# Shifting one key chunk of every second tile from TensorE's transposes to the DMA transposes, with the keys stored in load order

## The chip, the cores and the metric

One core of a Trainium2 chip runs the whole kernel as one program. Its engines are TensorE (PE; its weight loads are PEld), VectorE (DVE), ScalarE (ACT), GpSimd (POOL) and SyncE (SP), which here only issues DMAs. The metric is device time in microseconds. The kernel before took 1773.42 us (median of three runs, 1768.99 to 1776.42).

## The reference

Two stages follow each other. The first is attention of 49152 query rows (4 batches of 12288, 128 channels) over 768 keys per batch, which are 4 x 4 means of a larger array, projected; keys and values are the same rows. The second is a mixture of eight experts: a skip score decides which rows are computed, the best of eight logits chooses the expert, and two products (128 to 1024 to 128) with a ReLU between them are scaled and added to the row.

```python
kv_flat = kv.reshape(B, H // 4, 4, W // 4, 4, C).mean(axis=(2, 4)).reshape(B, -1, C) @ w_sr
k = v = kv_flat
a = softmax(q @ k.transpose(0, 2, 1) / sqrt(C))       # 12288 x 768 per batch
x = (a @ v).reshape(B * S, C)
do_compute = x @ w_skip > 0
e_idx = argmax(xc @ w_gate)                           # xc: the rows with do_compute
h = maximum(xc[mask] @ w1[e], 0.0)
y[mask] = gate_w[mask, None] * (h @ w2[e])
out[do_compute] = xc + y                              # other rows: out = x
```

## The kernel before

**Attention** runs over 384 tiles of 128 queries, 96 to a batch. The keys of a batch stand in six chunks of 128. One step `t` of the loop issues work of several tiles at once, and every engine executes its instructions in the order in which the step lists them:

- `p_transpose(t - 2)`, then `scores(t)`: six products of 384 columns, L637 to L639, which stand for one product of the scores in three parts (high by high, high by low, low by high);
- `attend(t - 10)`: 18 products of 138 columns, L700. Each needs a transposed 128 x 128 block of the tile's probabilities as its weights, for six key chunks, a high and a low part of each;
- `row_max(t)` on VectorE (L645), `row_exp(t)` on ScalarE (L650), and `p_hi(t - 1)` on ScalarE (L654) and `p_lo(t - 1)` on VectorE (L658), which split the probabilities of some chunks into two f16 parts.

The transposed probabilities come by two ways. The first `KD = 4` key chunks are split in SBUF (`p16`, 128 x 1024 f16) and transposed by one DMA per tile, which SyncE issues at L661 into `pt`. The other two chunks are transposed by TensorE in f32 (L674, two 128 x 128 products for a tile). Two tiles (`PP = 2`) share one PSUM bank for that, and it is split into `ptq` once for the pair, on ScalarE (L682) and VectorE (L683). `attend` takes its weights from `pt` and `ptq`. It runs ten steps after the scores (`LAG = 10`); `ptp` has 10 buffers for `pt`, `hl` 9 for `p16`, `ptq` 6.

**The keys of the next batch** are loaded while a batch is worked on. Each of the six chunks takes four loads of 256 KB (128 partitions of 2 KB): one plain load that SyncE issues (L448) and three that GpSimd issues and that add to what is there (L450). `KV_T` spreads the 24 loads over the first 75 tiles of a batch. GpSimd then adds up the rest (L476, L479), and `prep_kv` projects the keys. The keys of the first batch are loaded ahead of the loop, 24 plain loads, which VectorE (L463) and GpSimd pool as they land.

**SyncE's queue** holds, in program order, the DMA transposes, the loads of the queries (L602, one for four tiles), the stores of the attention rows (L719, one for four tiles) and the plain key loads. GpSimd issues the adding key loads and the writes of routed rows into expert buckets (L194).

**The experts.** The first group of rows is worked on ahead of a loop (`peel`), from buffers that are named `up_ps` on TensorE. Then `n_it` is read (the number of iterations, L1063) and the loop of groups begins, whose first instruction on TensorE is L293.

The lines of the change and of the prediction's steps:

Of the kernel before, what the change touches and what calls it, by code (L numbers as in the profile page):

```python
# [9 lines left out]
F32 = mybir.dt.float32  # L10
F32R = mybir.dt.float32r
BF16 = mybir.dt.bfloat16
F16 = mybir.dt.float16
# [11 lines left out]
def kernel(  # L25
# [11 lines left out]
    nc = tc.nc  # L37
    NR, C, RT, P = q.shape
    B = kv.shape[0]
    NQ = NR * RT * P // B  # L40
    H, W = kv.shape[1], kv.shape[2]
    R = 4
    NK = (H // R) * (W // R)
    KC = NK // P
# [24 lines left out]
    W1, W2, W3 = 3, 6, 0  # L69
    PSL = 11  # L70
    KD = 4
    PP = 2
# [334 lines left out]
    with ExitStack() as p1:  # L407
# [31 lines left out]
        W8 = W // R  # L439
        HG = P // W8  # L440
# [211 lines left out]
        def p_hi(t):  # L652
            P16[t] = hl.tile([P, 2, KD * P], F16, name="p16")
            nc.scalar.activation(out=P16[t][:, 0, :], in_=p_flat(t)[:, 0:KD * P], func=AF.Copy, scale=2.0 ** PEXP)  # L654

        def p_lo(t):
            p16 = P16.pop(t)
            LO[:] = [nc.vector.scalar_tensor_tensor(out=p16[:, 1, :], in0=p_flat(t)[:, 0:KD * P], scalar=2.0 ** PEXP,  # L658
                                                    in1=p16[:, 0, :], op0=ALU.mult, op1=ALU.subtract).ins]
            PT[t] = ptp.tile([P, 2 * KD, P], F16, name="pt")  # L660
            nc.sync.dma_start_transpose(PT[t], p16.rearrange("p a x -> p (a x)"))  # L661
# [4 lines left out]
        KP = KC - KD  # L666

        def p_transpose(t):
            g, j = divmod(t, PP)
            if j == 0:  # L670
                PTP[g] = acc_ps()
            p = p_flat(t)
            for i in range(KP):
                nc.tensor.transpose(PTP[g][:, (j * KP + i) * P:(j * KP + i + 1) * P],  # L674
                                    p[:, (KD + i) * P:(KD + i + 1) * P], ident)
            P_SB.pop(t)
            if j < PP - 1:
                return
            ps = PTP[g][:, 0:PP * KP * P]
            hl_t = ptq.tile([P, 2, PP * KP * P], F16, name="ptq")  # L680
            PTQ[g] = hl_t.rearrange("p a (j k x) -> p a j k x", j=PP, x=P)
# [6 lines left out]
        def attend(t):  # L688
# [8 lines left out]
            ptq_t = PTQ[t // PP]  # L697
            for i, (k, a, x) in enumerate(AVL):
                w = pt[:, x * KD + k, :] if k < KD else ptq_t[:, x, t % PP, k - KD, :]
                nc.tensor.matmul(ps[:, j % 2, :], w, v[a][:, k, :], start=(i == 0), stop=(i == len(AVL) - 1))  # L700
# [362 lines left out]
        n_it = nc.values_load(cumi[0:1, 0:1], min_val=1, max_val=NG + 1)  # L1063

# [70 lines left out]
```

## Time and profile before

| | |
|---|---|
| median of the runs | 1773.42 us |
| profiled execution | 1778.48 us, of which the traced span is 1776.7 |
| TensorE busy | 1721.4 us, 97% |
| VectorE, ScalarE, GpSimd busy | 85%, 74%, 36% |
| attention tiles | about 40 to 992 us |
| first group of the experts | 992 to 1026 us |
| loop over groups | from 1028 us |

The profile is one execution. Its matmuls overlap, so their durations add up to more than the time that they take: what one product costs TensorE is read from the distance between starts. "DMA share" is the time of all packets over the time of 16 DMA engines. It goes over 1.00 where an engine works on several packets at once, so that 1.00 is not its limit. A DMA's duration in the SyncE rows is the time of its issue: it grows where SyncE has to wait until the queue takes more.

### The profile page before, as it was taken

Reading aid. Unit: us, or ns where it says so; the run is one execution under the profiler, and the core shown is the slowest. Engines: PE = TensorE matmul, PEld = TensorE weight load, DVE = VectorE, ACT = ScalarE, POOL = GpSimd, SP = SyncE. Lnnn points to the kernel's source line nnn. Section 1 sums busy time; section 2 is a strip of 40 time slices with the busy share of each in tenths; the row PEclk is TensorE's granted clock in tenths of the full one; section 3 lists DMA queues with packets and bytes.
Section 4 is the critical chain, followed back from the end, with each engine's and each line's share of the span. In section 5 each row is a group of like instructions: output and inputs, shape, how many; then the busy total and the mean of one; then the engine's idle time right before and its main releaser. Section 6 shows DMA issues by size and latency. Waiting matters only on the chain. (4 is left out here: it accounts for less than half of the span.)

```text
span 1776.7 us, 41426 instructions
## 1 busy us (share of the span) xinstructions
PE 1721.4 (97%) x13906; PEld 1240.2 (70%) x13906; DVE 1502.7 (85%) x3181; ACT 1317.0 (74%) x2487; POOL 632.0 (36%) x799
## 2 busy tenths in 40 slices
PE   3999999999999999999999999999999999999997
PEld 2899989999899999999988544444444444444443
DVE  6888889899899988999999678888888788888886
ACT  2888888888888888888898456666666666666664
POOL 3233423444334344232332133333333333333333
PEclk9999999999999999999999999999999999999999
DMA  7999999999999999999999233333333433333333
GB/s 186 181 209 216 219 212 234 223 215 202 223 226 226 202 230 235 210 167 231 231 182 207 78 102 96 96 96 101 101 98 98 101 97 96 97 104 99 98 103 82
DMA packets 609811, 284.83 MB, mean 160 GB/s; under 512 B 495616, under 2 KB 564352, under 8 KB 609664
## 3 DMA queue, kind: packets, MB, share of 16 engines
q1 hardware_dynamic: 588064, 222.76, 63.9%
q0 software_dynamic: 21600, 60.19, 12.9%
q8 instruction: 83, 1.36, 0.3%
q14 instruction: 64, 0.52, 0.1%
HBM read 90.47 MB, written 72.30 MB: 92 GB/s over the span
## 5 line engine op out<-in xcount | busy, mean ns | idle before, releaser
L297 DVE SCALAR_TENSOR_TENSOR h_lo<-h_ps,h_hi 128x512 f16<-128x512 f32 x544 | 344.1, 685 | 134.9 <-ACT h_hi L296 134.9
L186 POOL DMA_INDIRECT out_dram<-o,ids x288 | 283.2, 983 | 478.9 <-DVE o L328 410.1
L650 ACT ACTIVATE p_sb<-s_ps,nm 128x768 f32<-128x768 f32 x384 | 347.4, 905 | 115.8 <-DVE nm L645 112.9
L645 DVE TENSOR_REDUCE nm<-s_ps 128x1 f32<-128x768 f32 x384 | 365.2, 951 | 69.7 <-PE s_ps L639 66.3
L296 ACT ACTIVATE h_hi<-h_ps 128x512 f16<-128x512 f32 x544 | 318.1, 597 | 49.7 <-PE h_ps L295 30.2
L700 PE MATMUL acc_ps<-v_hi,pt 128*128 128x138 f16 x3072 | 320.1, 224 | 5.3 <-DMA pt<-p 5.1
L700 PEld LDWEIGHTS <-pt 128*128 128x128 f16 x4608 | 275.2, 97 | 67.5 <-issue 55.7
L700 PE MATMUL acc_ps<-v_lo,pt 128*128 128x138 f16 x1536 | 293.0, 223 | 0.0
L637 PE MATMUL s_ps<-k_hi,q_hi 128*128 128x384 f32 x768 | 291.8, 380 | 0.0
L658 DVE SCALAR_TENSOR_TENSOR p<-p_sb,p 128x512 f16<-128x512 f32 x384 | 273.7, 713 | 3.0 <-ACT p L654 2.7
L619 POOL TENSOR_TENSOR q_lo<-q_sb,q_hi 128x256 fp32r<-128x256 f32 (+1 forms) x190 | 147.8, 779 | 327.2 <-DVE p L658 195.6
L639 PE MATMUL s_ps<-k_hi,q_lo 128*128 128x384 f32 x768 | 258.9, 337 | 0.0
L638 PE MATMUL s_ps<-k_lo,q_hi 128*128 128x384 f32 x768 | 258.0, 336 | 0.0
L654 ACT ACTIVATE p<-p_sb 128x512 f16<-128x512 f32 x384 | 243.1, 633 | 10.1 <-DMA pt<-p 7.3
L293 PE MATMUL h_ps<-xT,w_hi 128*128 128x512 f16 x544 | 207.1, 381 | 2.7 <-issue 2.7
L294 PE MATMUL h_ps<-xT,w_hi 128*128 128x512 f16 x544 | 207.2, 381 | 0.0
L295 PE MATMUL h_ps<-xT,w_lo 128*128 128x512 f16 x544 | 207.1, 381 | 0.0
L309 PEld LDWEIGHTS <-w_hi 128*128 128x128 f16 x1152 | 112.7, 98 | 134.9 <-issue 1.5
L309 PE MATMUL y_ps<-h_hi,w_hi 128*128 128x512 f16 x544 | 206.2, 379 | 0.0
L309 PE MATMUL y_ps<-h_hi,w_lo 128*128 128x512 f16 x544 | 206.2, 379 | 0.0
L312 ACT ACTIVATE yT<-y_ps,y_sc 128x512 f32<-128x512 f32 x68 | 46.7, 687 | 214.7 <-PE y_ps L309 155.7
L309 PE MATMUL y_ps<-h_lo,w_hi 128*128 128x512 f16 x544 | 195.1, 379 | 0.0
(214 smaller groups left out, 2932.1 us busy)
## 6 DMA issues: line engine op xcount, KB each, us to landing
q_sb<-in_q_dram SPq DMA_DIRECT2D x96, 256.0 KB, 4.8
out_dram<-rows SPq DMA_DIRECT2D x96, 256.0 KB, 3.7
xin<-scr SPq DMA_DIRECT2D x75, 276.0 KB, 3.0
w_raw<-in_moe_w_dram SPq DMA_DIRECT2D x34, 512.0 KB, 3.8
kvt<-in_kv_dram POOLq DMA_DIRECT2D x54, 256.0 KB, 5.8
kvt<-in_kv_dram SPq DMA_DIRECT2D x42, 256.0 KB, 5.4
pt<-p SPq DMA_TRANSPOSE x384, 4.7
out_dram<-o,ids POOLq DMA_INDIRECT x288, 2.7
```

Source lines behind the costliest of these rows:

```text
L186: ins = nc.gpsimd.indirect_dma_start(out=dst, out_offset=bass.IndirectOffsetOnAxis(ap=ids, axis=0), in_=src, in_offset=None, bounds_check= ...
L296: nc.scalar.activation(out=h["hi"][:, c, :], in_=ps, func=AF.Relu)
L297: nc.vector.scalar_tensor_tensor(out=h["lo"][:, c, :], in0=ps, scalar=0.0, in1=h["hi"][:, c, :], op0=ALU.max, op1=ALU.subtract)
L309: nc.tensor.matmul(ps, w[:, c, :], h[x][:, c, :], start=(i == 0), stop=(i == len(terms) - 1))
L637: nc.tensor.matmul(s[:, h, :HK], q_hi, k_hi[:, sl], start=True, stop=False)
L638: nc.tensor.matmul(s[:, h, :HK], q_hi, k_lo[:, sl], start=False, stop=False)
L639: nc.tensor.matmul(s[:, h, :HK], q_lo, k_hi[:, sl], start=False, stop=True)
L645: nc.vector.tensor_reduce(out=NM[t], in_=S_PS[t][:, :, :HK], axis=AX.XY, op=ALU.max, negate=True)
L650: nc.scalar.activation(out=P_SB[t], in_=S_PS.pop(t)[:, :, :HK], func=AF.Exp, bias=NM.pop(t))
L654: nc.scalar.activation(out=P16[t][:, 0, :], in_=p_flat(t)[:, 0:KD * P], func=AF.Copy, scale=2.0 ** PEXP)
L658: LO[:] = [nc.vector.scalar_tensor_tensor(out=p16[:, 1, :], in0=p_flat(t)[:, 0:KD * P], scalar=2.0 ** PEXP, in1=p16[:, 0, :], op0=ALU.mult ...
L700: nc.tensor.matmul(ps[:, j % 2, :], w, v[a][:, k, :], start=(i == 0), stop=(i == len(AVL) - 1))
```

## The change

Three things are changed together.

1. `KD` becomes `(4, 5)`. Even tiles keep four chunks on the DMA transpose and two on TensorE. Odd tiles have five on the DMA (a DMA transpose of ten 128 x 128 blocks and no longer eight) and one on TensorE. A pair has three TensorE transposes where it had four, and the bank that it shares is split in 384 columns, not 512. The split of the fifth chunk moves into `p_hi` and `p_lo` of the odd tile, which get 640 columns, not 512. `ptq` has five buffers, not six.
2. The key array is stored in DRAM in the order of its loads: one load reads one contiguous piece of 256 KB, where it read 16 pieces of 16 KB, 64 KB apart. The four buffers of the key loads become two new ones and the two `yT` tiles, which the experts use later.
3. Four products of 512 columns are issued on TensorE between the reading of `n_it` and the loop. Their result isn't used.

```diff
-    W1, W2, W3 = 3, 6, 0
+    W1, W2, W3, W4 = 3, 6, 0, 4
-    KD = 4
-    PP = 2
+    KD = (4, 5)
+    PP = len(KD)
...
         def load_kv(b, k, rs=range(R)):
             if rs[0] == 0:
-                KVT[b, k] = (kv_first if b == 0 else kvp).tile([P, R if b == 0 else 1, R * C], F32, name="kvt")
-            src = kv[b, k * HG * R:(k + 1) * HG * R].rearrange("(i r) (g w) c -> r i g (w c)", r=R, w=R)
+                KVT[b, k] = kv_first.tile([P, R, R * C], F32, name="kvt") if b == 0 else kv_next[k % len(kv_next)]
             for r in rs:
                 if b == 0 or r == 0:
-                    nc.sync.dma_start(KVT[b, k][:, r, :], src[r])
+                    nc.sync.dma_start(KVT[b, k][:, r, :], kv[b, k, r])
                 else:
-                    nc.gpsimd.dma_start(KVT[b, k][:, 0, :], src[r], accum_op=ALU.add)
+                    nc.gpsimd.dma_start(KVT[b, k][:, 0, :], kv[b, k, r], accum_op=ALU.add)
...
         def p_hi(t):
-            P16[t] = hl.tile([P, 2, KD * P], F16, name="p16")
-            nc.scalar.activation(out=P16[t][:, 0, :], in_=p_flat(t)[:, 0:KD * P], func=AF.Copy, scale=2.0 ** PEXP)
+            n = KD[t % PP] * P
+            P16[t] = hl.tile([P, 2 * max(KD) * P], F16, name="p16")[:, 0:2 * n].rearrange("p (a x) -> p a x", a=2)
+            nc.scalar.activation(out=P16[t][:, 0, :], in_=p_flat(t)[:, 0:n], func=AF.Copy, scale=2.0 ** PEXP)
...
-            PT[t] = ptp.tile([P, 2 * KD, P], F16, name="pt")
+            PT[t] = ptp.tile([P, 2 * max(KD), P], F16, name="pt")[:, 0:2 * kd, :]
             nc.sync.dma_start_transpose(PT[t], p16.rearrange("p a x -> p (a x)"))
...
-        KP = KC - KD
+        KP = [sum(KC - x for x in KD[:j]) for j in range(PP + 1)]
...
-            for i in range(KP):
-                nc.tensor.transpose(PTP[g][:, (j * KP + i) * P:(j * KP + i + 1) * P],
-                                    p[:, (KD + i) * P:(KD + i + 1) * P], ident)
+            for i in range(KP[j], KP[j + 1]):
+                k = KD[j] + i - KP[j]
+                nc.tensor.transpose(PTP[g][:, i * P:(i + 1) * P], p[:, k * P:(k + 1) * P], ident)
...
-                w = pt[:, x * KD + k, :] if k < KD else ptq_t[:, x, t % PP, k - KD, :]
+                w = pt[:, x * kd + k, :] if k < kd else ptq_t[:, x, KP[t % PP] + k - kd, :]
...
-        ptq = p1.enter_context(tc.tile_pool(name="ptq", bufs=6))
+        ptq = p1.enter_context(tc.tile_pool(name="ptq", bufs=5))
-        kvp = p_kv.enter_context(tc.tile_pool(name="kvp", bufs=4))
+        kvp = p_kv.enter_context(tc.tile_pool(name="kvp", bufs=2))
+        kv_next = [x.unsqueeze(1) for x in yTs] + [kvp.tile([P, 1, R * C], F32, name="kvt") for _ in range(2)]
...
         n_it = nc.values_load(cumi[0:1, 0:1], min_val=1, max_val=NG + 1)
+        idle = alloc["h"]()
+        for _ in range(W4):
+            nc.tensor.matmul(idle, w1_hi[:, 0:P], h["hi"][:, 0, :], start=True, stop=True)
...
+        if name == "kv":
+            b, h, w, c = a.shape
+            rows = 128 // (w // 4)
+            a = a.reshape(b, -1, rows, 4, w // 4, 4 * c).transpose(0, 1, 3, 2, 4, 5).reshape(b, -1, 4, 128, 4 * c)
```

On SyncE, a stretch of the first batch (`pt<-p` is a DMA transpose from `p16`, its last numbers are partitions, blocks and columns), before:

```order
L661 DMA_TRANSPOSE pt<-p_1174 128x8x128
L661 DMA_TRANSPOSE pt<-p_1216 128x8x128
L602 DMA q_sb<-in_q_dram 128x512
L661 DMA_TRANSPOSE pt<-p_1261 128x8x128
L719 DMA out_dram<-rows 128x4x128
L661 DMA_TRANSPOSE pt<-p_1305 128x8x128
L448 DMA kvt<-in_kv_dram 128x1x512
```

The same stretch with the change:

```order
L657 DMA_TRANSPOSE pt<-p_1163 128x8x128
L657 DMA_TRANSPOSE pt<-p_1205 128x10x128
L596 DMA q_sb<-in_q_dram 128x512
L657 DMA_TRANSPOSE pt<-p_1249 128x8x128
L716 DMA out_dram<-rows 128x4x128
L657 DMA_TRANSPOSE pt<-p_1293 128x10x128
L442 DMA kvt<-in_kv_dram 128x512
```

Nothing has changed its place; every second transpose has grown by two blocks of 128 x 128.

On TensorE, the end of `attend` of an odd tile and what follows it (`acc_ps<-ident,p_sb` is a TensorE transpose), before:

```order
L700 LDWEIGHTS ptq
L700 MATMUL acc_ps<-v_hi,ptq 128x138
L700 LDWEIGHTS ptq
L700 MATMUL acc_ps<-v_hi,ptq 128x138
L700 LDWEIGHTS ptq
L700 MATMUL acc_ps<-v_lo,ptq 128x138
L674 MATMUL acc_ps<-ident,p_sb 128x128 x2
```

For the odd tiles the transposes stand as one product, and three of the weights come from `pt` instead of `ptq`; the step of an odd tile's transpose, with the change:

```order
L697 LDWEIGHTS ptq
L697 MATMUL acc_ps<-v_lo,ptq 128x138
L671 MATMUL acc_ps<-ident,p_sb 128x128
L631 MATMUL s_ps<-k_hi,q_hi 128x384
L632 MATMUL s_ps<-k_lo,q_hi 128x384
```

The 18 products of `attend` stay 18; 192 of 768 TensorE transposes are gone.

On TensorE at the entry of the loop over groups (`cumi` holds `n_it`), with the change:

```order
L306 MATMUL acc_ps<-h_lo,w_hi 128x512
L1064 LDWEIGHTS w_hi
L1061 TENSOR_LOAD cumi
L1064 MATMUL up_ps<-h_hi,w_hi 128x512
L1064 LDWEIGHTS w_hi
L1064 MATMUL up_ps<-h_hi,w_hi 128x512
...
L1077 COMPARE_AND_BRANCH
L1077 UNCONDITIONAL_BRANCH
L1136 BRANCH_PREFETCH_HINT
L290 LDWEIGHTS w_hi
```

Before, the load of `cumi` is followed by the branch at once; four products now stand between them.

## Rows read from the trace of the kernel before

**Rows 1.** Stretches by batch (columns stand in the first line).
```profile
core 0: us, PE busy (x) PEld busy (x) DVE busy (x) ACT busy (x) POOL busy (x), PEclk, DMA share, GB/s
57.00:290.00 233.00, 231.35 (x2529) 215.32 (x2527) 203.31 (x392) 201.43 (x372) 83.83 (x116) 1.00 1.17 216
290.00:527.00 237.00, 232.78 (x2542) 215.98 (x2541) 211.56 (x407) 202.25 (x376) 91.53 (x128) 1.00 1.15 217
758.00:992.00 234.00, 231.17 (x2497) 207.79 (x2497) 209.64 (x440) 196.93 (x380) 63.72 (x88) 1.00 0.97 192
```

**Rows 2.** Timeline of TensorE, batch 0: start, us, engine, line, operation, count, idle before.
```profile
222.53 0.39 PE L674 MATMUL acc_ps<-ident,p_sb 128*128 128x128 f32 x2
222.67 0.42 PE L637 MATMUL s_ps<-k_hi,q_hi 128*128 128x384 f32 x1
222.93 0.33 PE L638 MATMUL s_ps<-k_lo,q_hi 128*128 128x384 f32 x1
223.10 0.33 PE L639 MATMUL s_ps<-k_hi,q_lo 128*128 128x384 f32 x1
...
225.32 0.29 PE L700 MATMUL acc_ps<-v_hi,pt 128*128 128x138 f16 x2 [1.37 <-DMA pt<-p]
```

**Rows 3.** DMA queues and issues, 60 to 720 us: packets, MB, share; count, median us.
```profile
q1 hardware_dynamic: 335719, 112.03, 94.0%
q0 software_dynamic: 10368, 30.59, 21.1%
...
q_sb<-in_q_dram SPq DMA_DIRECT2D x68, 256.0 KB, 4.3
...
pt<-p SPq DMA_TRANSPOSE x273, 4.9
kvt<-in_kv_dram SPq DMA_DIRECT2D x16, 256.0 KB, 5.0
```

**Rows 4.** SyncE's waits for split probabilities: first 60 to 720 us, then 720 to 970.
```profile
SPq L661 <- DVE p L658: 5.3, 7, 1.3
...
SPq L661 <- DVE p L658: 26.3, 26, 2.5
```

**Rows 5.** Instructions on `pt` (12 products per tile) up to 225 and 758 us.
```profile
0.00:225.00 225.00, 62.57 (x840) 50.02 (x840) 1.00 1.08 203
...
0.00:758.00 758.00, 257.42 (x3456) 205.81 (x3456) 1.00 1.12 215
```

**Rows 6.** DMA transposes issued up to 225 and 758 us.
```profile
pt<-p SPq DMA_TRANSPOSE x72, 4.9
...
pt<-p SPq DMA_TRANSPOSE x296, 4.8
```

**Rows 7.** DMA from 940 to 960 us: GB/s in 40 slices, stores, transposes.
```profile
GB/s 195 191 143 8 9 182 325 315 216 203 228 206 177 224 206 148 215 201 157 214 188 199 263 199 184 0 7 53 282 292 282 263 170 214 203 254 279 212 209 218
...
out_dram<-rows SPq DMA_DIRECT2D x3, 256.0 KB, 3.5
pt<-p SPq DMA_TRANSPOSE x12, 4.2
```

**Rows 8.** VectorE's split by form, 60 to 720 us: shapes, count, busy us, mean ns.
```profile
L658 DVE SCALAR_TENSOR_TENSOR p<-p_sb,p 128x512 f16<-128x512 f32 x272 | 195.4, 718 | 2.6 <-ACT p L654 2.3 <-ACT p_sb L650 0.3
```

**Rows 9.** Start: key loads fill 8 to 27 us, query loads 28 to 30.
```profile
8.00:27.00 19.00, 4.74 (x12) 2.37 (x12) 16.03 (x15) 1.42 (x4) 5.42 (x10) 1.00 1.06 265
28.00:30.00 2.00, 1.30 (x5) 0.67 (x5) 1.97 (x2) 0.98 (x3) 0.01 (x1) 1.00 1.04 383
```

**Rows 10.** Timeline of the start: VectorE's poolings that waited for a key load.
```profile
12.72 3.58 DVE L463 TENSOR_REDUCE w_raw<-kvt 128x128 f32<-128x2048 f32 x1 [1.05 <-DMA kvt<-in_kv_dram]
...
22.57 1.91 DVE L463 TENSOR_REDUCE part<-kvt 128x128 f32<-128x1024 f32 x1 [1.68 <-DMA kvt<-in_kv_dram]
```

**Rows 11.** Stretches at the entry of the loop over groups.
```profile
1025.70:1028.20 2.50, 0.00 (x0) 0.00 (x0) 0.00 (x0) 0.69 (x1) 1.97 (x2) 0.67 0.41 108
1028.30:1033.30 5.00, 4.98 (x12) 1.82 (x13) 1.70 (x3) 1.79 (x3) 0.98 (x1) 0.50 0.38 131
```

More of the change, by code (lines that the diff above doesn't have):

```diff
@@ L38 @@
     NR, C, RT, P = q.shape
-    B = kv.shape[0]
+    B, KC, R = kv.shape[0:3]
     NQ = NR * RT * P // B
[L41 to L44, printed above, removed]
+    NK = KC * P
     NT = B * NQ
@@ L438 @@
         pooled, KV, KVT, PTB = {}, {}, {}, {}
-        W8 = W // R
-        HG = P // W8
         def load_kv(b, k, rs=range(R)):
             if rs[0] == 0:
-                KVT[b, k] = (kv_first if b == 0 else kvp).tile([P, R if b == 0 else 1, R * C], F32, name="kvt")
-            src = kv[b, k * HG * R:(k + 1) * HG * R].rearrange("(i r) (g w) c -> r i g (w c)", r=R, w=R)
+                KVT[b, k] = kv_first.tile([P, R, R * C], F32, name="kvt") if b == 0 else kv_next[k % len(kv_next)]
             for r in rs:
                 if b == 0 or r == 0:
-                    nc.sync.dma_start(KVT[b, k][:, r, :], src[r])
+                    nc.sync.dma_start(KVT[b, k][:, r, :], kv[b, k, r])
                 else:
-                    nc.gpsimd.dma_start(KVT[b, k][:, 0, :], src[r], accum_op=ALU.add)
+                    nc.gpsimd.dma_start(KVT[b, k][:, 0, :], kv[b, k, r], accum_op=ALU.add)
         def pooled_out(b, k):
@@ L652, in p_hi @@
         def p_hi(t):
-            P16[t] = hl.tile([P, 2, KD * P], F16, name="p16")
-            nc.scalar.activation(out=P16[t][:, 0, :], in_=p_flat(t)[:, 0:KD * P], func=AF.Copy, scale=2.0 ** PEXP)
+            n = KD[t % PP] * P
+            P16[t] = hl.tile([P, 2 * max(KD) * P], F16, name="p16")[:, 0:2 * n].rearrange("p (a x) -> p a x", a=2)
+            nc.scalar.activation(out=P16[t][:, 0, :], in_=p_flat(t)[:, 0:n], func=AF.Copy, scale=2.0 ** PEXP)
         def p_lo(t):
             p16 = P16.pop(t)
-            LO[:] = [nc.vector.scalar_tensor_tensor(out=p16[:, 1, :], in0=p_flat(t)[:, 0:KD * P], scalar=2.0 ** PEXP,
+            kd = KD[t % PP]
+            LO[:] = [nc.vector.scalar_tensor_tensor(out=p16[:, 1, :], in0=p_flat(t)[:, 0:kd * P], scalar=2.0 ** PEXP,
                                                     in1=p16[:, 0, :], op0=ALU.mult, op1=ALU.subtract).ins]
-            PT[t] = ptp.tile([P, 2 * KD, P], F16, name="pt")
+            PT[t] = ptp.tile([P, 2 * max(KD), P], F16, name="pt")[:, 0:2 * kd, :]
             nc.sync.dma_start_transpose(PT[t], p16.rearrange("p a x -> p (a x)"))
@@ L678, in p_transpose @@
                 return
-            ps = PTP[g][:, 0:PP * KP * P]
-            hl_t = ptq.tile([P, 2, PP * KP * P], F16, name="ptq")
-            PTQ[g] = hl_t.rearrange("p a (j k x) -> p a j k x", j=PP, x=P)
+            ps = PTP[g][:, 0:KP[PP] * P]
+            hl_t = ptq.tile([P, 2, KP[PP] * P], F16, name="ptq")
+            PTQ[g] = hl_t.rearrange("p a (k x) -> p a k x", x=P)
             split_a.append(lambda: nc.scalar.activation(out=hl_t[:, 0, :], in_=ps, func=AF.Copy, scale=2.0 ** PEXP))
@@ L697, in attend @@
             ptq_t = PTQ[t // PP]
+            kd = KD[t % PP]
             for i, (k, a, x) in enumerate(AVL):
-                w = pt[:, x * KD + k, :] if k < KD else ptq_t[:, x, t % PP, k - KD, :]
+                w = pt[:, x * kd + k, :] if k < kd else ptq_t[:, x, KP[t % PP] + k - kd, :]
                 nc.tensor.matmul(ps[:, j % 2, :], w, v[a][:, k, :], start=(i == 0), stop=(i == len(AVL) - 1))
```

## The prediction

> **What bounds the kernel now.** I read the page's busy shares first, then busy time by stage, then the DMA queues and SyncE's waits, and last the timeline where TensorE stops. TensorE is the busy engine: over the first batch it works 231.35 of 233.00 us, over the second 232.78 of 237.00 [rows 1]. VectorE and ScalarE have 10 to 15% left. So a shorter stream of products looks worth its full length. But in the same rows the DMA share is 1.17 and 1.15 in the batches beside which keys are loaded, and 0.97 in the last one, where none are. Since the share can go over one, the question is whether 1.15 is a full queue. Three readings say that it is. From 60 to 720 us the transposes on SyncE waited for their split probabilities 5.3 us in all, against 26.3 us in the shorter stretch without key loads [rows 4]: before 720 us there is always a transpose ready, and SyncE waits for the queue. Second, the lead: up to 225 us 72 transposes are issued and 840 / 12 = 70 tiles consumed, a lead of two tiles; up to 758 us it is 296 against 3456 / 12 = 288, a lead of eight [rows 5, 6]. Third, with that lead of two TensorE stops 1.37 us for `pt` [rows 2]. So through three of four batches two streams run side by side, each nearly full: TensorE, and the DMA engines. The change takes from the first and gives to the second.
>
> **TensorE's part.** Two transposes and the first score product take 222.53 to 222.93 = 0.40 us from start to start, and the next score product 222.93 to 223.10 = 0.17 [rows 2]. That leaves 0.23 for two, so a transpose is 0.11 us. 192 go: 192 x 0.11 = 21 us, 16 in the first three batches and 5 in the last. The products of `attend` stay as many.
>
> **The splits.** The 512-column split is 718 ns on VectorE [rows 8]. The odd tile's gets 128 columns more, a quarter: between 0 and 0.18 us; the pair's split loses 128 of 512 columns, by the same bounds. ScalarE does likewise. I take zero for both together, since as many columns come as go, and both engines have idle time in these batches [rows 1]. The smaller counts of buffers cost nothing either: a pair's `ptq` is written three steps after its first tile and read until step 11, which is four and a half pairs for five buffers, and the key loads still have four.
>
> **The DMA's part.** An odd tile's transpose grows by two blocks, 256 rows of 256 bytes, 64 KB. From below: the fastest slice of half a microsecond moved 325 GB/s, so 64 KB cost at least 0.20 us [rows 7]. From above: in the same 20 us 12 transposes and 3 stores went through a queue that was full for most of it; a 256 KB store at 383 GB/s [rows 9] is 0.68 us, which leaves (20 - 2.1) / 12 = 1.50 us for eight blocks, 0.37 us for two. I take 0.31, nearer to the upper end, because that row holds whole transposes beside other traffic. In the first three batches there are 144 odd tiles: 45 us of DMA time (29 to 53). In the last batch 48 odd tiles cost 15 us, and SyncE has 26.3 us of waits to put them in [rows 4].
>
> The Trainium skill (DMA: Bandwidth & Descriptors, "Latency and other measured facts") gives a DMA transpose 261 GB/s with a non-contiguous middle dimension and 350 to 400 without. By that page 64 KB would be an estimated 0.25 or about 0.17 us, and the 144 tiles 36 or 25 us. The row above, 256 KB in 1.50 us, is 175 GB/s and slower than both.
>
> **What the DMA has left.** Before the queue comes too late for TensorE, it can lose its lead: six tiles (eight less two) at 660 us / 273 transposes = 2.42 us [rows 3] are 14.5 us, and the 5.3 us of SyncE's waits, together 20 us.
>
> **The keys' layout.** At the start, 8 to 27 us, key loads alone fill the queue at 265 GB/s; the query loads right behind them, also 128 runs of 2 KB, get 383 [rows 9]. So the old order of the keys is slow when nothing else runs, and 256 KB would take 0.68 and not 0.99 us. In the loop, 72 loads run in the first three batches. The most that they can give back is the same 0.31 us each, 22 us; the least is nothing. There the keys are a small part of the 143 MB that move, spread between transposes, and the plain key loads land in 5.0 us where the well laid out queries land in 4.3 [rows 3]. I take 5 us.
>
> The same section of the Trainium skill says that a row pitch of a large power of two slows a DMA from HBM, and that a contiguous layout cures it. Its pitches begin at 512 KiB; the one here is 64 KB, and the 265 against 383 GB/s agree in direction. If the rule held for the loop's loads as fully as at the start, it would give the 22 us of the bound above, and the sum would be about -6.
>
> At the start itself VectorE waits 1.05 and 1.68 us for later key loads [rows 10], and its first four loads, 1 MB, would take 2.7 us at 383 GB/s and not 4.0 at 265: together 4 us (0 to 5). The rest there is VectorE's own pooling, 16.03 of 19 us busy [rows 9].
>
> **The loop's entry.** TensorE has nothing for 2.50 us, its granted clock is 0.67 over that stretch and 0.50 for the 5.00 us behind it, the lower of its two levels (1.2 of 2.4 GHz), and 12 products take 4.98 us there [rows 11], where a clock of 1.00 would halve it. At half of 4.98 / 12 us each, four products fill some 0.83 us of the 2.50. If the clock stays up, 2.5 us come back; if they only delay the loop, 0.8 is lost. I take 1 us gained.
>
> **The sum,** against the profiled execution (1778.48 us, span 1776.7, 5.1 above the median of 1773.42). First three batches: 45 added, 5 given back by the layout, 20 taken from the lead and the waits, so tile 288 is 20 us later. The 16 us that TensorE saves there show nowhere: it waits for `pt` instead, at the first L700 of a step, with the next tile's transposes and scores queued behind. On SyncE the query loads, the stores and the plain key loads stand behind the longer transposes, and none of them is needed as soon as `pt`. The start gives 4, the last batch 4 of its 5, the entry 1. Together +11 us: 1789.5 for such an execution, 1784 for the median. Bounds: with 0.20 us, 22 from the layout and the upper gains elsewhere, -13 - 5 - 5 - 2.5 = about -25; with 0.37, nothing from the layout, start or last batch, +33 + 1 = about +34.
>
> **The rivals.** *The queue keeps up, and the kernel is faster.* Place: the odd tiles' transposes in batches 0 to 2. Price: 64 KB at 0.20 to 0.25 us, the key loads 0.2 to 0.3 us shorter. It decides from the point where 144 x price - layout is below the 20 us in hand; then TensorE's 16 us come out, with 5, 4 and 1 from the other places less what is still waited: some 20 us, 1753. For it: the 325 GB/s slice, and the start's 265 against 383. Against it: accumulating key loads are three of four and issue from another queue, where no row shows a well laid out one; and TensorE waits for `pt` already.
>
> *The two balance.* Price near 0.26 and some 12 us from the layout: 37 - 12 - 20 = 5 later at tile 288, and 9 come back at the start, in the last batch and at the entry: 1770, within 0.5% of before.
>
> *The queue is hit harder.* At 0.37 us and with a layout that does nothing in the loop: 53 - 20 = 33 later, less 4 to 8: some 27 up, 1800. For it: the price read off row 7 itself; against it, that row's queue was partly fed by what came before.
>
> **How the numbers follow.** Half a per cent, 8.9 us, is about what a measurement can tell from no change. My forecast of a DMA-bound loss of 9 to 20 us has a chance of 0.33, the harder hit 0.12, the balance 0.28, the faster rival 0.27. Slower is the sum of the first two. The forecast's own range is 1782 to 1794; with the others, until 2 in 10 are left out, 1756 to 1803.
>
> **What the profile after would show.** If I am right, the DMA share in all first three batches is as high as 1.17, SyncE's waits for split probabilities before 720 us are near zero, and TensorE's idle time, 1.7 and 4.2 us in the first two [rows 1], is some 10 to 20 us a batch, and most of it at L700 in the second half of a batch. The plain key loads at the start run near 383 GB/s and the first scores come some 4 us earlier. At the entry the granted clock is 1.00 soon after the branch, or the idle products did nothing. I would be wrong if the lead at the end of the third batch is again seven or eight tiles: then the two added blocks cost less than 0.25 us, or the key loads gave back far more than 5 us, which the time of the adding loads to landing would tell apart.

## The result and the profile after

The changed kernel took 1790.28 us (median of 11 runs, 1784.08 to 1796.80), the kernel before 1775.65 in the same runs (1768.99 to 1783.03). The ratio is 1.0086, with a 95% interval of 1.0065 to 1.0108: slower by some 15 us, as forecast, and by less than 2%. The forecast was 1784 us, in a range of 1756 to 1803, with a chance of 0.45 for slower. The profiled execution took 1795.57 us (span 1793.8), 5 above its median.

These are the stretches of [rows 1] with the change, and the third batch between them (columns as there). The last batch begins later now, so its own stretch stands below the four:

```profile
57.00:290.00 233.00, 225.58 (x2446) 208.53 (x2445) 204.63 (x388) 197.33 (x367) 83.48 (x115) 0.99 1.15 222
290.00:527.00 237.00, 225.96 (x2403) 207.56 (x2401) 206.61 (x393) 194.57 (x363) 90.61 (x124) 0.98 1.15 221
527.00:758.00 231.00, 217.81 (x2321) 200.31 (x2319) 198.56 (x381) 187.26 (x349) 88.25 (x123) 0.98 1.16 221
758.00:992.00 234.00, 229.47 (x2507) 210.62 (x2506) 222.72 (x456) 207.21 (x398) 68.18 (x94) 1.00 1.12 219
...
781.00:1014.00 233.00, 228.47 (x2459) 203.88 (x2457) 212.34 (x444) 196.60 (x382) 62.76 (x88) 1.00 1.05 207
```

The third batch before:

```profile
527.00:758.00 231.00, 231.00 (x2529) 215.23 (x2526) 207.44 (x405) 201.53 (x374) 90.12 (x126) 1.00 1.14 220
```

TensorE was idle for 1.7, 4.2 and 0.0 us in the first three batches, and now for 7.4, 11.0 and 13.2. The DMA share has not risen there. It is 1.15 to 1.16 where it was 1.14 to 1.17, and the rate is 221 or 222 GB/s where it was 216 to 220: a queue that was full can't get fuller, so the added blocks show as time. Only the last batch had room, and went from 0.97 to 1.05.

What TensorE waits for, 60 to 720 us, first before and then with the change (busy us, mean ns of one | idle time ahead, and what ended it):

```profile
L700 PE MATMUL acc_ps<-v_hi,pt 128*128 128x138 f16 x2170 | 226.2, 224 | 5.3 <-DMA pt<-p 5.1
```

```profile
L697 PE MATMUL acc_ps<-v_hi,pt 128*128 128x138 f16 x2350 | 244.4, 226 | 27.3 <-DMA pt<-p 26.7
```

That is 26.7 us instead of 5.1 of waiting for transposed probabilities. ScalarE waits for transposes too: its split stood for 28.7 us, before for 7.3, until a transpose had freed a `p16` buffer.

SyncE's row for the split probabilities, 5.3 us before [rows 4], is gone in the same stretch, and after 720 us 7.3 us are left of 26.3 (waiting instruction, what it waited for: us in total, times, longest):

```profile
SPq L657 <- DVE p L654: 7.3, 8, 2.6
```

So the waiting has changed sides: before 720 us no transpose waits for its source any more, and TensorE waits for transposes.

One set of rows could mislead here. From 60 to 720 us the profile puts 364 us of SyncE's transposes down to TensorE, 172.4 of them to L697, whose products free the `pt` buffers (before, 369 us). By the times of the products, those that free a transpose's buffer had ended at least 7 us before its issue, every time, and at least 4 us in the trace of before. So these are not waits for TensorE; they are the time of the issue itself, which is 1.23 us at its shortest in either trace and 5.1 us, with the change 6.8, at its longest.

The DMA of [rows 3] (60 to 720 us), with the change:

```profile
q1 hardware_dynamic: 349700, 114.45, 93.5%
q0 software_dynamic: 10368, 30.59, 20.9%
...
q_sb<-in_q_dram SPq DMA_DIRECT2D x64, 256.0 KB, 4.2
...
pt<-p SPq DMA_TRANSPOSE x257, 4.9
```

The same 94% of the engines' time held 273 transposes of eight blocks, 2184 blocks, and now holds 257 of nine on average, 2313, with four query loads fewer. More blocks pass, but fewer tiles.

The lead of the transposes over TensorE is read as in [rows 5, 6] (a pair of tiles now has 12 + 15 = 27 products on `pt`), up to 225 and 780.6 us. First the products, then the transposes issued:

```profile
0.00:225.00 225.00, 69.54 (x956) 56.97 (x957) 1.00 1.05 214
...
0.00:780.60 780.60, 287.41 (x3888) 235.32 (x3888) 0.98 1.12 220
```

```profile
pt<-p SPq DMA_TRANSPOSE x73, 5.3
...
pt<-p SPq DMA_TRANSPOSE x295, 4.8
```

At 225 us it is 73 less 956 / 27 x 2 = 70.8, two tiles. At 780.6 us, where tile 288 begins, it is 295 - 288 = seven. Tile 288 began at 758.2 us before, so 22.4 us went by then, although the lead has come back.

Loads at the start, against [rows 9]:

```profile
12.00:24.00 12.00, 3.90 (x9) 1.81 (x9) 11.82 (x13) 1.53 (x4) 5.44 (x10) 1.00 1.05 392
```

The key loads now run at 392 GB/s, where the old order had 265. VectorE is busy for 11.82 of the 12 us, and the first product of `attend` starts at 53.0 us instead of 56.9 in these two traces.

At the entry of the loop over groups, TensorE's timeline (start, duration, ..., idle time ahead in brackets) and the stretches that answer to [rows 11] are:

```profile
1045.82 1.02 PE L1064 MATMUL up_ps<-h_hi,w_hi 128*128 128x512 f16 x4 [0.49 <-issue]
1047.93 0.38 PE L290 MATMUL h_ps<-xT,w_hi 128*128 128x512 f16 x1 [1.09 <-issue]
```

```profile
1045.30:1047.80 2.50, 1.05 (x5) 0.29 (x3) 0.00 (x0) 0.69 (x1) 1.95 (x2) 1.00 0.46 116
1047.90:1052.90 5.00, 4.97 (x26) 2.55 (x26) 3.00 (x5) 3.86 (x7) 0.98 (x1) 1.00 0.43 134
```

Here the clock stays at 1.00, and 26 products run in 5 us where 12 did. From the entry to the end of the trace it is 745.9 us, before 748.4.

Put together, from the list of starts of the products of `attend`: start -3.9 us, first to 288th tile +26.4 (701.3 to 727.6), last batch and first group -2.9 (270.2 to 267.3), loop -2.5. The sum is +17.1, the difference of the spans.

### The profile page after: what moved, and what is told of

Its sections match the earlier page's. It is cut to its first block, busy times and chain, and to the rows that moved or that the text cites. A ratio compares the mean times of both kernels' runs of the same rounds, so it can differ in the third digit from the quotient of the medians.

```text
span 1793.8 us, 41083 instructions
## 1 busy us (share of the span) xinstructions
PE 1715.8 (96%) x13718; PEld 1229.9 (69%) x13718; DVE 1515.0 (84%) x3181; ACT 1311.8 (73%) x2487; POOL 635.0 (35%) x799
## 3 DMA queue, kind: packets, MB, share of 16 engines
q0 software_dynamic: 21600, 60.19, 12.6%
## 4 chain that ended last, share of the span: by engine, by line
PE 77%; DMA 9%; DVE 9%; issue 2%; ACT 2%; POOL 0%; SPq 0%; POOLq 0%; DVEq 0%; another core or an unknown queue 0%; ACTq 0%
PE y_ps L306 20%; PE acc_ps L697 17%; DMA pt<-p 8%; PE h_ps L290 7%; PE h_ps L292 7%; PE h_ps L291 7%; PE s_ps L631 5%; PE s_ps L632 5%; PE s_ps L633 5%; DVE nm L639 3%; PE acc_ps L671 3%; PE x_ps L314 2%; DVE p L654 1%; DMA kvt<-in_kv_dram 1%; ACT p_sb L644 1%
## 5 line engine op out<-in xcount | busy, mean ns | idle before, releaser
L697 PE MATMUL acc_ps<-v_hi,pt 128*128 128x138 f16 x3456 | 358.4, 225 | 30.5 <-DMA pt<-p 29.9
L697 PEld LDWEIGHTS <-pt 128*128 128x128 f16 x5184 | 313.4, 98 | 96.9 <-issue 54.8
L697 PE MATMUL acc_ps<-v_lo,pt 128*128 128x138 f16 x1728 | 330.8, 224 | 0.0
L654 DVE SCALAR_TENSOR_TENSOR p<-p_sb,p 128x512 f16<-128x512 f32 (+1 forms) x384 | 304.6, 793 | 15.0 <-ACT p L649 14.6
L649 ACT ACTIVATE p<-p_sb 128x512 f16<-128x512 f32 (+1 forms) x384 | 264.8, 690 | 34.6 <-DMA pt<-p 31.9
L290 PE MATMUL h_ps<-xT,w_hi 128*128 128x512 f16 x544 | 206.2, 379 | 1.1 <-issue 1.1
```

Source lines behind the costliest of these rows:

```text
L290: nc.tensor.matmul(ps, w1_hi[:, sl], hi, start=True, stop=False)
```

## The experiments

The theory: a full DMA queue takes all that the fifth chunk adds in the first three batches, and TensorE's saving can't show there. The first rival: what is slower is something else (the clock, the buffers, VectorE's longer split), and the DMA only looks busy. The second: the parts of the change are each a little good or bad, and the layout or the idle products decide.

**Each part alone.** The fifth chunk without the layout and without the idle products:

```diff
+            src = kv[b, k * HG * R:(k + 1) * HG * R].rearrange("(i r) (g w) c -> r i g (w c)", r=R, w=R)
...
-                    nc.sync.dma_start(KVT[b, k][:, r, :], kv[b, k, r])
+                    nc.sync.dma_start(KVT[b, k][:, r, :], src[r])
...
-                    nc.gpsimd.dma_start(KVT[b, k][:, 0, :], kv[b, k, r], accum_op=ALU.add)
+                    nc.gpsimd.dma_start(KVT[b, k][:, 0, :], src[r], accum_op=ALU.add)
...
-        for _ in range(W4):
-            nc.tensor.matmul(idle, w1_hi[:, 0:P], h["hi"][:, 0, :], start=True, stop=True)
```

> Only the fifth chunk of odd tiles goes to the DMA; the keys keep their old order and no idle products are issued. If the DMA queue is the bound, this is the changed kernel without its helpers: some 4 us at the start and 2.5 at the loop's entry are missing, and the key loads in the loop give nothing back, so 7 to 15 us above the changed kernel, 20 to 30 above before (ratio 1.011 to 1.017), with SyncE's waits for split probabilities from 60 to 720 us under 1 us. If the loss came from the new key layout or the shared key buffers instead, this kernel is at or below before, since TensorE has 21 us less to do.

Measured: 1.0152 (1.0105 to 1.0199), inside what the theory gave, and slower than the whole change. SyncE's waits for split probabilities from 60 to 720 us are 1.7 us, where under 1 was expected. Three kernels then add parts to the kernel before: the new layout alone, the idle products alone (the lines of the diff of the change), and both. Of the layout's edit:

```diff
-                    nc.sync.dma_start(KVT[b, k][:, r, :], src[r])
+                    nc.sync.dma_start(KVT[b, k][:, r, :], kv[b, k, r])
...
-                    nc.gpsimd.dma_start(KVT[b, k][:, 0, :], src[r], accum_op=ALU.add)
+                    nc.gpsimd.dma_start(KVT[b, k][:, 0, :], kv[b, k, r], accum_op=ALU.add)
```

> Only the order of the keys in DRAM. DMA theory: 4 us at the start, and in the loop at most the 6 us that TensorE stood idle in the first three batches: 1766 to 1772, ratio 0.994 to 0.998. The rival, by which the layout relieves the loop much more (22 us of DMA time), would show the lead of issued over consumed transposes at 225 and 456 us at six or more tiles instead of two or three. If the layout itself costs something in the loop, the time is at or above before.

> Only the four idle products at the loop's entry. If they keep the clock up: 2.5 us less, ratio 0.9986, granted clock 1.00 from the first product of the loop on. If they only delay the branch: 0.8 us more.

> Layout and idle products together, four chunks by DMA in all tiles. If the parts add up: 6.5 to 12 us below before, ratio 0.993 to 0.996, and 20 to 27 us below the changed kernel, all of which the fifth chunk costs. If the changed kernel's loss is not the fifth chunk, this one is near the changed kernel.

Measured: the layout 0.9958 (0.9934 to 0.9982), the idle products 0.9998 (0.9971 to 1.0026), both 0.9957 (0.9932 to 0.9982). The layout is worth 0.4%, the idle products nothing that these runs can tell from no change. The whole change against the last one: 1.0086 / 0.9957 = 1.013, so the fifth chunk costs some 23 us, and the layout hides a part of it. What the layout does in the loop is in SyncE's row for the split probabilities, 60 to 720 us, of the kernel with the layout alone:

```profile
SPq L655 <- DVE p L652: 19.3, 24, 1.7
```

That is 19.3 us against 5.3 [rows 4]. TensorE's waits for `pt` are gone in that trace, and it goes from the first to the 288th tile in 694.0 us, before in 701.3. The trace with layout and idle products, which is the same up to the loop, doesn't show it:

```profile
SPq L655 <- DVE p L652: 3.3, 6, 0.9
```

```profile
L694 PE MATMUL acc_ps<-v_hi,pt 128*128 128x138 f16 x2144 | 224.7, 225 | 11.6 <-DMA pt<-p 10.6 <-DVE nm L639 1.0
```

It takes 710.7 us for the same tiles, in the slowest execution of its 13 (1781.98 us, the median 1767.83). So one trace can differ from another by 17 us in these batches. The expectation named a sign for a relief of 22 us, a lead of six tiles or more at 225 and at 456 us: with the layout alone it is six and three.

**Room in the queue.** If the queue is the cause, traffic that is taken away elsewhere must bring the change's gain to light. Both kernels were run without the stores of the attention rows in the first three batches (72 of 96 stores, 18.9 MB; these rows are written only where the experts write them):

```diff
-                nc.sync.dma_start(ov[r][:, o * GT:(o + 1) * GT, :], rows[:, :, 0:C])
+                if t // TPB == B - 1:
+                    nc.sync.dma_start(ov[r][:, o * GT:(o + 1) * GT, :], rows[:, :, 0:C])
```

> The kernel before without the stores of attention rows in the first three batches (72 of 96 stores of 256 KB; those rows of the output stay unwritten where the experts don't write them). It only serves as a base for the next one. DMA theory: some 50 us of queue time go, SyncE's waits for split probabilities from 60 to 720 us rise from 2 to 5 us to over 25, TensorE no longer waits for pt, and since TensorE is then the bound the time falls only by what it stood idle: 3 to 8 us, ratio 0.995 to 0.998.

> The changed kernel without the same 72 stores. DMA theory: with 50 us of queue time free and some 35 added, TensorE is the bound again and the 192 transposes it no longer does come out: 15 to 25 us below before (ratio 0.986 to 0.992) and 10 to 20 below the kernel with fewer stores and four chunks. If a transpose of ten blocks is slow by itself, or the five ptq buffers or the wider splits hold the engines up, this kernel stays at or above the four-chunk one with fewer stores, whatever the queue has free.

Measured: the kernel before 0.9969 (0.9940 to 0.9997), the changed one 0.9883 (0.9828 to 0.9937; four runs, 1757 to 1767 us). With room, the whole change is a gain: 0.9883 / 0.9969 = 0.991, 15 us. Without these stores, SyncE's waits for split probabilities (60 to 720 us) are, before and with the change:

```profile
SPq L661 <- DVE p L658: 94.7, 107, 2.4
```

```profile
SPq L657 <- DVE p L654: 27.0, 30, 2.3
```

and in the changed kernel TensorE's idle time at L697 in the same stretch is:

```profile
L697 PE MATMUL acc_ps<-v_hi,pt 128*128 128x138 f16 x2512 | 257.7, 224 | 0.3
```

That is 0.3 us instead of 27.3, with nothing changed but the stores. It rules out the buffers, the splits and VectorE, which are the same in both. Two things have to be added.

A store takes SyncE's time to issue as well as the transfer's, so these runs alone don't tell which of the two is full. The transposes of the kernel before, 60 to 720 us, shortest, median and longest issue in ns:

```profile
L661 SPq DMA_TRANSPOSE pt<-p x273: 1232/1437/5071, 58.8 to 719.8; - x137
```

At their shortest, 273 issues take 336 of the 660 us, and SyncE's loads and stores some 60 more. So SyncE's issuing alone doesn't fill the stretch; what holds it up stands behind it. How much of a longer issue is SyncE's own, no row tells.

And a wait of SyncE isn't room in the queue one for one. Its waits fell from 94.7 to 27.0 us, by 68, while 144 x 0.2 us of added blocks (the price found below) and 12 us of shorter time make 41.

**TensorE's saving.** In the changed kernel TensorE does the second transpose of the odd tiles again, into a part of the bank that nobody reads:

```diff
+            if j == 1:
+                nc.tensor.transpose(PTP[g][:, 3 * P:4 * P], p[:, 4 * P:5 * P], ident)
```

> The changed kernel in which TensorE still does the second transpose of each odd tile, into a part of the bank that nobody reads: the DMA's load of the change without TensorE's relief. DMA theory: the relief shows only where TensorE is the bound (the first forty tiles, the last batch), so this is 4 to 9 us above the changed kernel, ratio to before 1.010 to 1.014. If TensorE's time decided throughout, it would be 21 us above, ratio 1.020.

Measured: 1.0089 (1.0058 to 1.0121), where the change has 1.0086. All 192 transposes that the change removes are back, and the time is the same within the intervals. It came out just below the expected 1.010 to 1.014, of which the interval holds the lower half; it excludes the 1.020 of a kernel in which TensorE's time decides throughout. One thing was different in its trace, though: the granted clock, which in the result's trace falls six times in the first three batches (the last section shows it), falls once here, and these batches take 716.7 us from first to 288th tile where they took 727.6. So a part of the loss might be the clock's. To tell, the unused transposes were put into the first three batches alone, and the change was run again in the same set:

```diff
-            if j == 1:
+            if j == 1 and t < 288:
```

> The changed kernel, in which TensorE does the second transpose of odd tiles again in the first three batches alone, unused. It fills 144 x 0.11 = 16 us of TensorE's waits there, and leaves the last batch as it is. If only the queue sets the time of these batches, the ratio is that of the change in the same set, within 0.002. If the falls of the clock behind long waits cost up to 10 us and a fuller TensorE has one of them and not six, it is 0.004 to 0.005 lower than the change.

> The changed kernel itself, in the same set as the one with the unused transposes in three batches, to be compared with it. Ratio to before 1.0065 to 1.0108 by its first runs. The falls of the clock in attention should be there again, four to six; if there are one or none, the trace of the result was not typical of the change, and they are no part of the loss.

Measured: 1.0095 (1.0065 to 1.0125) with them, 1.0100 (1.0072 to 1.0129) for the change itself. From first to 288th tile it is 722.3 us with one fall, 720.8 with three. So the falls show no cost; but the two traces differ by two falls, not by the five of the expectation, and a cost of a few us would not be seen. Another comparison weighs more: with one fall the three batches took 716.7 and 722.3 us, 15 and 21 more than the 701.3 of before. Most of the loss is there without the falls. A trace of the change differs from another by 7 us in these batches (720.8 and 727.6), and one with the layout by 17 (694.0 and 710.7, above), which has to be kept in mind below. TensorE's waits, 60 to 720 us, with the unused transposes in three batches and for the change beside it:

```profile
L699 PE MATMUL acc_ps<-v_hi,pt 128*128 128x138 f16 x2367 | 243.5, 224 | 19.8 <-DMA pt<-p 19.4
```

```profile
L697 PE MATMUL acc_ps<-v_hi,pt 128*128 128x138 f16 x2368 | 244.4, 225 | 28.2 <-DMA pt<-p 27.8
```

What TensorE does more, it waits less, and the same number of products, 2367 and 2368, stands in the same time.

**Twice the dose.** All tiles have five chunks on the DMA:

```diff
-    KD = (4, 5)
+    KD = (5, 5)
```

> The fifth chunk on the DMA for even tiles too: twice the added blocks (288 odd and even tiles in the first three batches, not 144), TensorE has two transposes fewer a pair. Theory as predicted (0.31 us for two blocks, 20 us of reserve already spent by the first dose): the second 144 tiles cost the full 45 us, the last batch runs out of its 26 us of SyncE waits and loses 0 to 4: ratio to before 1.031 to 1.036. Corrected theory (0.22 to 0.25 us for two blocks, hardly any reserve, 5 us from the layout): the second dose costs 32 to 36 us, as the first did: ratio 1.027 to 1.030. Rival, that the first dose hurt mostly by short falls of the clock after waits and not by queue time: the second dose adds under 20 us, ratio below 1.020.

Measured: 1.0308 (1.0285 to 1.0330), 1.022 times the change, some 39 us. The total lies on the border of the two theories, and far from the third; the trace tells where it goes. Products on `pt` from 57 to 758 us, in the kernel before (12 for a tile), with the fifth chunk alone (13.5 on average), with the whole change in the result's trace and in the one of its last run (13.5) and with five chunks for all (15):

```profile
57.00:758.00 701.00, 257.31 (x3456) 205.70 (x3454) 1.00 1.15 218
```

```profile
57.00:758.00 701.00, 275.31 (x3714) 225.52 (x3714) 0.98 1.16 221
```

```profile
57.00:758.00 701.00, 276.50 (x3738) 226.39 (x3738) 0.98 1.15 222
```

```profile
57.00:758.00 701.00, 276.24 (x3771) 225.81 (x3767) 0.99 1.15 224
```

```profile
57.00:758.00 701.00, 291.52 (x4035) 243.02 (x4035) 0.99 1.16 227
```

That is 288, 275.1, 276.9, 279.3 and 269.0 tiles, or 2.434, 2.548, 2.532, 2.510 and 2.606 us for one. Every second tile grew each time. With the old layout two blocks cost (2.548 - 2.434) x 2 = 0.23 us, and more if a reserve took up a part of it. Between the change and the double dose no reserve is left (SyncE waits for no split probabilities in either, 60 to 720 us), and there they cost (2.606 - 2.532) x 2 = 0.15 us by the one trace and (2.606 - 2.510) x 2 = 0.19 by the other; the two traces with the unused transposes, whose DMA is that of the change, give 0.21 and 0.17 by their times to the 288th tile. So the price is some 0.2 us (0.15 to 0.23), and not 0.31. What makes the double dose dear is the last batch. Its 95 tiles take 243 us there, against 230 with the change, and its DMA share is 1.14:

```profile
800.00:1033.00 233.00, 215.67 (x2300) 194.49 (x2299) 205.40 (x426) 190.73 (x370) 64.64 (x88) 0.98 1.14 226
```

TensorE is idle for 17 us of that stretch. Ten blocks in every tile fill the queue even where no keys are loaded.

**Only where there is room.** Since only the last batch had room, two kernels have the new layout, the idle products and four chunks in the first three batches. In the last batch the one has five chunks in odd tiles, the other in all. Both have one key buffer fewer than the change:

```diff
+    FIVE = range(3 * 96, 4 * 96)
...
+        def chunks(t):
+            return KD[t % PP] if t in FIVE else KD[0]      # the other: KD[1] if t in FIVE
```

> New key layout, idle products, and five chunks by DMA only in the odd tiles of the last batch, where no key loads run (one key buffer fewer, for space). DMA theory: the last batch has the queue time, so TensorE's 5 us come out, 3 to 5 us below the kernel with layout and idle products alone: 1763 to 1766, ratio 0.992 to 0.994. If the queue is short there too, or the missing key buffer costs, it is at 0.996 or above.

> Five chunks for all tiles of the last batch and four in the first three, new key layout, idle products: 96 DMA transposes of ten blocks where no keys are loaded. If two blocks cost 0.22 to 0.25 us, 96 of them are 21 to 24 us of queue time against 26 us of SyncE's waits there, and TensorE saves 96 x 2 x 0.11 / 2 = 10 us: ratio 0.989 to 0.992. If they cost 0.31 us, 30 us don't fit into 26, and the gain is that of five chunks in odd tiles alone or less: 0.994 to 0.997.

Measured: 0.9945 (0.9921 to 0.9970) and 0.9993 (0.9974 to 1.0011). The first is the lowest ratio of all complete kernels and beats the kernel before by 0.5% and the change by 1.4%. Whether it beats the layout alone (0.9958) the intervals don't tell. The second loses that again. Both came out above what I expected, the first by little (0.992 to 0.994), the second above either of its ranges. The last batch of either, from its first tile on:

```profile
747.00:980.00 233.00, 228.45 (x2462) 204.05 (x2461) 212.28 (x444) 196.73 (x381) 62.60 (x88) 1.00 1.04 207
```

```profile
747.00:980.00 233.00, 220.44 (x2353) 197.31 (x2351) 204.57 (x431) 191.94 (x374) 65.97 (x88) 0.99 1.08 218
```

TensorE is idle for 4.6 us with the one and 12.6 with the other. I had expected 21 to 24 us of blocks to fit into 26 us of SyncE's waits, and by the price of 0.2 us they are only 19. SyncE's waits for split probabilities, 747 to 980 us, with five chunks in odd tiles and in all:

```profile
SPq L658 <- DVE p L655: 6.9, 8, 2.6
```

```profile
SPq L658 <- DVE p L655: 1.5, 2, 1.2
```

With the second the waits are used up nearly to the end, though 96 x 0.2 us should have left some. What TensorE waits for there:

```profile
PE acc_ps L677 <- ACT p_sb L645: 7.0, 8, 2.6
PE acc_ps L703 <- DMA pt<-p: 3.1, 2, 2.2
```

Only 3.1 us of its idle time is for transposed probabilities; 7.0 are for ScalarE's exponentials. ScalarE itself waits 4.4 us there until a transpose has freed a `p16` buffer, and 5.8 us for transposed rows of the experts, which SyncE issues as well; with five chunks in odd tiles neither wait is in its list. So a late transpose seems to reach TensorE by a second way, through ScalarE; no run tests that. What the runs do show is that 26 us of SyncE's waits were not 26 us of room.

## Why the prediction came out right, and which terms were off

**The bound** was right: through three batches the DMA queue was full, and the saving on TensorE fell where nothing waits for it. The experiments show it from three sides (the saving taken back, the queue relieved, the dose doubled), and two of the signs that the prediction named came: share as high as before, SyncE's waits gone. The third, 10 to 20 us of idle TensorE a batch, came smaller, at 7.4 to 13.2, most of it at the first product on `pt`. It did not come in the second half of each batch: the first batch has all of its 7.4 us there, but the second has 7.2 of 11.0 in its first half and the third 6.8 of 13.2.

**The price of two blocks** was too high: 0.31 us, and the runs show 0.15 to 0.23, around the lower bound of 0.20. Its upper end of 0.37 came from 20 us with 12 transposes [rows 7], taken as a queue that was full for most of it. That row has slices of 8, 9, 0 and 7 GB/s in it. A rate that is taken over a stretch with holes gives the price of the holes too. But five slices under 60 GB/s are only some 2.3 us; without them the row still gives (20 - 2.1 - 2.3) / 12 = 1.30 us for eight blocks, 0.33 for two. The rest of the way to 0.2 is another error: the price was taken as a quarter of a transpose of eight blocks, and by these numbers two blocks that are added to one cost less than that. What else a transpose costs, no row shows. The Trainium skill (DMA: Bandwidth & Descriptors, "Latency and other measured facts") has 261 or 350 to 400 GB/s for a DMA transpose, an estimated 0.25 or 0.17 us for the 64 KB. The measured 0.15 to 0.23 us agree with that page better than the row that I preferred.

**The reserve** was too large: 20 us, six tiles of lead and 5.3 of SyncE's waits. In the trace of the fifth chunk alone, the first 288 tiles take 732.8 us against 701.3, 31.5 more. By the price between the change and the double dose, 0.15 to 0.21 us, 144 odd tiles are 22 to 30 us, no more than was lost. So no reserve shows, as far as traces that differ by 7 to 17 us can tell; 20 us would have shown. The lead of eight tiles that I counted at 758 us isn't something that a batch carries to the next. It is built anew in the last two dozen tiles of each batch, when the key loads have stopped: in the trace of before it stands at 7 to 8 there, and at 3 to 5 in the second half of every batch up to that point, and the two tiles at 225 us that I took for its beginning are the bottom of such a swing. At 780.6 us it stands at seven again. The prediction named exactly that as the sign that would make it wrong, and its reading of the sign (the blocks cost less than 0.25 us) was right, while the reserve had to fall with it.

**The two errors cancel.** Predicted for the first three batches: 45 - 5 - 20 = 20 us. By the runs: 144 x 0.2 = 29, less 5 to 12 for the layout and next to nothing for the reserve, is 17 to 24, and the change's two traces have 26.4 (727.6) and 19.5 (720.8) more than the 701.3 of before. So the mechanism was right, and the sum came out by luck, from two wrong terms. The double dose, where they don't cancel, shows it: by the predicted terms 45 us more in these batches, and its trace has 747.5, which is 20 to 27 more than the change's.

**The layout**: at the start 3.9 us in the two traces of the result, where 4 was predicted. Over all traces it is less: the first product of `attend` starts at 54.3 to 56.9 us in the four with the old order and at 52.7 to 54.1 in the ten with the new, on average 2.4 us sooner. In the loop where the queue is full, the first 288 tiles take 732.8 us with the fifth chunk and the old layout, and 727.6 or 720.8 with the new: 5 to 12, where 5 was predicted. With four chunks, three of the four traces with the new layout have 14.2, 19.3 and 20.3 us of SyncE's waits from 60 to 720 us where 5.3 were, and take 7 to 8 us less for the first 288 tiles (694.1, 694.0 and 693.3 against 701.3). TensorE is the bound from there on: it takes 694.1 without the stores too. The fourth, the one of 710.7 us, has neither. So the layout may have freed more than the 5 us, up to the 22 of the bound if SyncE's waits were room one for one, which they are not. On the row-pitch rule of the same section of the Trainium skill: the start agrees in direction, 265 to 392 GB/s; how much of the full 22 us the loop gave back, these traces don't settle.

**TensorE's term** of 0.11 us a transpose was somewhat too high. It can be read in the first three batches of the two kernels without the stores, where TensorE is idle for less than 1 us: from the first tile to the 288th they take 694.1 and 681.9 us, 12.1 for 144 transposes, 0.08 each (predicted 16 for the 144). In the 95 tiles behind, 237.7 and 230.0 us, the first has a wait of 2.5 us for ScalarE with a fall of the clock behind it, so the difference there is not TensorE's saving alone.

**The last batch** gave 2.9 us together with the first group, predicted 4. **The entry** gave 2.5 us in the traces of the result, where I took 1 from a range that ended there. It is not bound to the change: the loop took 746.1 us in the trace of the layout alone, without idle products, and 747.6 with them in the one with unused transposes in three batches. The last section shows the clock falling in spite of them.

**The rivals.** "The queue keeps up" asked for a price of 0.20 to 0.25 us, which is about what it was, and still failed, because its other half, 20 us in hand, wasn't there. With the stores gone the changed kernel comes near its 1753 us: 1761.88. "Hit harder" (1800) failed by its price; "balance" (1770) by the same missing reserve.

## What to carry to other kernels

When two resources run side by side, each nearly full, work that is moved from the one to the other costs what the receiver pays. Ask first which of them has the waits. A lead of one stream over the other that comes and goes is a reserve only down from its lowest point in each period, not from the highest: here it was back at seven or eight tiles at the end of a batch, and down to two or three inside it, where TensorE waited already. A wait of the engine that issues transfers is no measure of the room in the queue. The price of a longer transfer is to be read from the difference of two rates, both from a full queue, and not as a share of a whole transfer; and one trace of each is little, where traces of the same code differ by 7 to 17 us.

## What the runs showed of the hardware that I had not expected

The granted clock fell within attention, which it did not in the trace of before. At six of the seven longest waits for `pt` in the result's trace it went to 0.50, the lower of its two levels (1.2 of 2.4 GHz), for 3.4 us, once 6.8. One of them, in TensorE's timeline and in stretches:

```profile
716.98 0.34 PE L633 MATMUL s_ps<-k_hi,q_lo 128*128 128x384 f32 x1
720.52 0.41 PE L697 MATMUL acc_ps<-v_hi,pt 128*128 128x138 f16 x2 [3.20 <-DMA pt<-p]
720.72 0.32 PE L697 MATMUL acc_ps<-v_lo,pt 128*128 128x138 f16 x1
```

```profile
713.00:719.90 6.90, 4.32 (x47) 3.84 (x44) 4.71 (x8) 3.78 (x8) 1.06 (x2) 1.00 1.08 181
719.90:723.30 3.40, 2.78 (x21) 2.79 (x22) 1.45 (x3) 2.34 (x5) 0.42 (x1) 0.50 1.18 191
723.30:730.00 6.70, 6.70 (x76) 6.22 (x75) 4.85 (x8) 5.08 (x10) 3.35 (x7) 1.00 1.16 222
```

The waits ahead of these falls were 2.3 to 3.7 us; the longest in attention before was 1.6. The length alone doesn't decide: in the change's last trace a wait of 3.2 us has no fall behind it, and in the one beside it a wait of 1.9 us has one. The 18 products behind one took 2.04 us (720.52 to 722.56), where those of another tile take 1.09 (712.54 to 713.63). What a fall costs the kernel, these runs don't tell: with one fall and with three the time was the same, as told above.

The entry of the loop has a wait of its own that the idle products don't govern. The runs were made in four sets, each on another chip. In the first and the last TensorE waited 1.1 to 2.7 us ahead of the loop's first product; in all six profiles of the two between, 6.8 to 8.2, with the idle products or without. The first row is the kernel before without the stores, which has no idle products, the second the one with five chunks in odd tiles of the last batch, which has four:

```profile
1028.82 0.59 PE L293 MATMUL h_ps<-xT,w_hi 128*128 128x512 f16 x1 [8.18 <-issue]
```

```profile
1020.46 0.59 PE L291 MATMUL h_ps<-xT,w_hi 128*128 128x512 f16 x1 [7.00 <-issue]
```

Both products take 0.59 us where 0.38 is usual [the row of L290 above]: the clock had fallen in the wait, and four products ahead of it could not keep it up. The kernel before took 1774.45 and 1772.46 us in the first and last set, 1778.66 and 1782.57 in the others, so times are compared here as ratios within a set. What the 7 us wait for, no row shows; it stays open, and set and chip can't be told apart.
